# Four u tiles from TensorE to the DMA crossbar, an earlier attention, and one load held back

## The chip, the cores and the metric

One core of a Trainium2 chip. The metric is the device time of one execution in microseconds (us), the median of several runs; each run is listed with its mean granted TensorE clock. A run over 1.5% above the fastest of its kernel counts as slow. A ratio is the mean time of one kernel's fast runs over that of the other's in the same rounds, so it is not quite the ratio of the medians quoted.

## The reference, cut to what matters

```
q, k, v: (8 batches, 8 heads, 576 positions, 64), float32
scores = q k^T / 8, causal, window of 64 positions; attn = softmax(scores); x = attn v      # (8, 576, 512)
h = x^T U V (rank 32);  u = x + h^T;  out = u + relu(u w_ch1) w_ch2                         # w_ch1: 512 x 2048
```

## The kernel before

The 4608 tokens are worked on in nine chunks of 512. Each chunk has 32 slots: slots 0 to 15 hold the first matrix product (`ch1`, one group of 16 x 128 hidden columns each), slots 16 to 31 the second (`ch2`). Into the slots of chunk c the kernel puts the attention and the low-rank part of batch c+1. `ch1` reads u transposed (`uTc`), so each 128 x 512 tile of u must be transposed before the next chunk begins: on TensorE for batches under `NXT`, else by the DMA crossbar, issued from SyncE.

```python
NXT = 3
...
def UT(t):                                   # transpose u tile t of batch b
    def f():
        g = g0 + t
        dst = uT_of(g // TPC)[:, g % TPC, :, :]
        if b >= NXT:
            nc.sync.dma_start_transpose(out=dst, in_=u_tiles[g][:])
            return
        tp = ps_tp.tile([P, NDC, P], BF16, name="tpu", tag="tp")
        for dc in range(NDC):
            nc.tensor.transpose(tp[:, dc, :], u_tiles[g][:, dc * P : (dc + 1) * P], ident[:])
        nc.scalar.copy(out=dst, in_=tp[:])
...
def loads(b, *tiles):                        # GpSimd: wait, then load V and K/Q
    for t in tiles:                          # reads tile t of batch b+1's transposed Q: waits until it has landed
        nc.gpsimd.tensor_copy(out=held[:], in_=qfs[(b + 1) % 2][0:1, t * HP * P : t * HP * P + 1])
    if b <= 2:
        load_v(b + 1)
    for _ in load_kq(b + 2, False):
        pass
...
if 2 < b and b + 1 < B:                      # head of chunk b-1
    if b > 3:
        nc.gpsimd.tensor_copy(out=held[:], in_=uT_of(c)[0:1, TPC - 1, 0, 0:1])
    load_v(b + 1)
if 2 < b and b + 2 < B:
    loads(b, 2)
...
CROSS = {0: {2: [16, 17, 18, 19, 20]}, 1: {3: [10, ..., 14], 4: [26, ..., 30]}, 2: {5: [24, ..., 28]}}
CROSS_N = [22, 23, 24, 25, 26]               # slots of the crossbar transposes of K/Q, per chunk and batch
```

All loads go out on GpSimd's queue in program order, all crossbar transposes and stores on SyncE's, in program order too.

The softmax here doesn't subtract the row's maximum and nothing guards it: scores larger than these inputs give would overflow.

## Time and profile before

| | before |
|---|---|
| median of the first runs | 311.0 us (310.54 to 311.38) |
| span of the profiled run | 310.6 us |
| TensorE busy / DMA in use | 97% / nearly full to about 200 us |
| chunk 1, chunk 2, chunk 3, chunk 4 (from the chain in order of time) | 33.37, 31.95, 31.83, 31.62 us |

The lines are in the prediction. The digits of the page are tenths busy in 40 slices of the span; in the busy times by stretch each engine has its busy us and, in brackets, its instructions. Names: `kr`, `qr` are the loaded K and Q, `kf`, `qf` the same transposed, `vA`, `vB` V; `un` is a u tile, `uTc` u transposed, `tpu` its transpose on TensorE; `psA`, `psU` are the first and second matrix product in PSUM. PE is TensorE, PEld its weight loads, DVE VectorE, ACT ScalarE, POOL GpSimd, SPq SyncE's queue.

### The profile page before, as it was taken

What the parts mean: (1) busy time and instruction counts of PE and PEld (TensorE: products, weight loads), DVE (VectorE), ACT (ScalarE), POOL (GpSimd) and SP (SyncE); (2) the same over time, 40 slices, a digit from 0 to 9 for tenths busy, and PEclk for the clock granted to TensorE, in tenths of its full rate; (3) what the DMA queues carried; (4) which work ended last, traced back from release to release, by engine and by line L of the source; (5) the groups of instructions that cost most, each with busy time, mean ns of one, the idle gap of its engine ahead of it and who ended that gap; (6) DMA issues with size and microseconds to landing.
All of it is one profiled execution on the core that took longest, in us unless ns stands there. A gap on an engine that the chain in (4) does not pass through costs nothing.

```text
span 310.6 us, 6952 instructions
## 1 busy us (share of the span) xinstructions
PE 301.8 (97%) x2881; PEld 147.6 (48%) x2903; DVE 175.1 (56%) x336; ACT 108.2 (35%) x173; POOL 102.0 (33%) x136
## 2 busy tenths in 40 slices
PE   7799999999999999999999999999999999999996
PEld 7453554544545544454445444544454444444443
DVE  4485566528667873677557765666566542116011
ACT  3555680358127620543044304440354004101500
POOL 8693264294695091437143705000000000000000
PEclk9999999999999999999999999999999999999999
DMA  7999999999999999999599999932400275011011
GB/s 107 170 209 208 204 172 145 147 148 160 138 148 157 139 142 203 130 156 172 103 150 141 184 118 132 175 103 74 132 2 0 68 222 203 32 69 36 0 65 70
DMA packets 156495, 39.87 MB, mean 128 GB/s; under 512 B 145040, under 2 KB 151440, under 8 KB 156464
## 3 DMA queue, kind: packets, MB, share of 16 engines
q0 software_dynamic: 104720, 18.88, 82.0%
q1 hardware_dynamic: 51744, 20.55, 34.0%
q8 instruction: 22, 0.36, 0.5%
q14 instruction: 9, 0.07, 0.1%
HBM read 37.97 MB, written 9.44 MB: 153 GB/s over the span
## 4 chain that ended last, share of the span: by engine, by line
PE 93%; DMA 3%; issue 1%; DVE 1%; POOL 1%; ACT 0%; POOLq 0%
PE psA L765 41%; PE psU L789 40%; DMA qr<-in_q_dram 3%; PE sc L347 3%; PE xw L409 2%; PE psv L660 2%; PE pshh L533 1%; PE tpu L694 1%; PE tpg L283 1%; PE low L347 0%; PE psh L533 0%; DVE xs L420 0%; POOL kr L120 0%; PE tpw L283 0%; PE xe L409 0%
## 5 line engine op out<-in xcount | busy, mean ns | idle before, releaser
L765 PE MATMUL psA<-uTc,w1b 128*128 128x512 bf16 (+1 forms) x584 | 131.2, 377 | 0.3 <-DVE uTc L635 0.3
L789 PE MATMUL psU<-w2b,c 128*128 128x512 bf16 (+2 forms) x572 | 127.3, 373 | 1.3 <-issue 0.3
L789 PEld LDWEIGHTS <-c 128*128 128x128 bf16 x592 | 56.0, 98 | 66.0 <-issue 2.9
L765 PEld LDWEIGHTS <-w1b 128*128 128x128 bf16 x584 | 54.3, 98 | 63.9 <-issue 2.6
L777 ACT ACTIVATE c<-psA 128x512 bf16<-128x512 f32 x84 | 50.1, 597 | 83.6 <-PE psA L765 83.3
L775 DVE TENSOR_SCALAR c<-psA 128x512 bf16<-128x512 f32 x60 | 41.3, 689 | 40.9 <-PE psA L765 40.9
L802 DVE TENSOR_TENSOR osb<-psU,un 128x512 f32<-128x512 f32 (+2 forms) x29 | 19.5, 671 | 52.4 <-PE psU L789 52.4
L367 ACT ACTIVATE pts<-sc 128x1024 bf16<-128x1024 f32 x32 | 31.3, 1028 | 2.3 <-PE sc L347 2.3
L138 POOL DMA_DIRECT2D vA<-in_v_dram x32 | 28.3, 913 | 7.4 <-DMA w1b<-in_moe_w_ch_dram 2.7
L675 DVE TENSOR_TENSOR un<-psv,xs 128x512 bf16<-128x512 f32 (+3 forms) x48 | 26.1, 593 | 4.3 <-PE psv L660 4.0
L129 POOL DMA_DIRECT2D qr<-in_q_dram x30 | 26.7, 888 | 4.1 <-PE tpg L283 1.7
L129 POOL DMA_DIRECT2D kr<-in_k_dram x30 | 26.6, 887 | 3.4 <-PE sc L347 2.0
L400 ACT ACTIVATE ptl<-low 128x256 bf16<-128x256 f32 x6 | 2.3, 384 | 61.0 <-PE high L347 61.0
L373 DVE TENSOR_TENSOR pts<-pts,maskA 128x1024 bf16<-128x1024 bf16 x28 | 19.1, 682 | 1.7 <-ACT pts L367 1.7
L500 DVE TENSOR_TENSOR xs<-xw,rcw 128x896 bf16<-128x896 f32 x14 | 15.3, 1091 | 0.5
L963 POOL COPY held<-qf 1x1 bf16<-1x1 bf16 x5 | 0.9, 178 | 42.9 <-DMA qf<-qr 42.9
L347 PEld LDWEIGHTS <-kf 64*64 64x64 bf16 x704 | 9.8, 107 | 7.3 <-issue 7.0
L347 PE MATMUL sc<-qf,kf 64*64 64x128 bf16 (+1 forms) x608 | 11.5, 212 | 0.5 <-DVE qf L300 0.3
L409 PEld LDWEIGHTS <-pts 128*64 128x64 bf16 x512 | 9.8, 110 | 3.5 <-issue 2.5
L697 ACT COPY uTc<-tpu 128x512 bf16<-128x512 bf16 x9 | 5.3, 586 | 11.4 <-PE tpu L694 11.4
L409 PE MATMUL xw<-vA,pts 128*64 128x65 bf16 x217 | 8.4, 195 | 0.0
L974 POOL COPY held<-uTc 1x1 bf16<-1x1 bf16 x3 | 0.5, 177 | 23.6 <-DMA uTc<-un 23.6
(125 smaller groups left out, 190.7 us busy)
## 6 DMA issues: line engine op xcount, KB each, us to landing
out_dram<-osb SPq DMA_DIRECT2D x27, 256.0 KB, 2.3
vA<-in_v_dram POOLq DMA_DIRECT2D x32, 128.0 KB, 6.4
kr<-in_k_dram POOLq DMA_DIRECT2D x24, 128.0 KB, 5.4
qr<-in_q_dram POOLq DMA_DIRECT2D x24, 128.0 KB, 5.5
w2b<-in_moe_w_ch_dram POOLq DMA_DIRECT2D x4, 512.0 KB, 15.8
out_dram<-late SPq DMA_DIRECT2D x8, 256.0 KB, 4.2
vB<-in_v_dram POOLq DMA_DIRECT2D x8, 128.0 KB, 8.8
w1b<-in_moe_w_ch_dram POOLq DMA_DIRECT2D x2, 512.0 KB, 11.1
```

The lines of the kernel that those rows point to most:

```text
L129: nc.gpsimd.dma_start(out=dst[0:rows, t, :, :], in_=src[b, :, t * P : t * P + rows, :].rearrange("h p d -> p h d"),)
L138: nc.gpsimd.dma_start(out=dst[:, :, 0:D], in_=v[b, :, lo : lo + P, :].rearrange("h p d -> p h d"))
L347: nc.tensor.matmul(sc[g][r0 : r0 + W, col * W : (col + n) * W], keys_of(j, u, rs), queries_of(j, blk, n, rs), start=not spare, stop=last o ...
L367: nc.scalar.activation(out=dst, in_=sc[:], func=ACT.Exp, scale=scale)
L373: nc.vector.tensor_tensor(out=dst, in0=dst, in1=maskA.rearrange("p g n w -> p g (n w)"), op=ALU.mult)
L409: nc.tensor.matmul(dst, pts[:, h // 2, h % 2, blk, :] if blk < NB - 1 else ptl[:, h // 2, h % 2, :], rhs, start=True, stop=True,)
L675: nc.vector.tensor_tensor(out=u_tiles[g][rs, cs], in0=ps[0][n][rs], in1=x[rs, t, :, :].rearrange("p h d -> p (h d)")[:, cs], op=ALU.add,)
L765: nc.tensor.matmul(ps[i][:, ts.start * P : ts.stop * P], w1b[:, dc, i * P : (i + 1) * P], uTc[:, ts, dc, :], start=(dc == 0), stop=(dc == ...
L775: nc.vector.tensor_relu(out=c1[i][:], in_=ps[i][:])
L777: nc.scalar.activation(out=c1[i][:], in_=ps[i][:], func=ACT.Relu)
L789: nc.tensor.matmul(acc[t][:, lo:hi], c1[i][:, t * P : (t + 1) * P], w2b[:, i, lo:hi], start=(i == 0), stop=(i == NFC - 1),)
L802: nc.vector.tensor_tensor(out=osb[:, lo:hi], in0=acc[t][:, lo:hi], in1=u_tiles[g][:, lo:hi], op=ALU.add,)
```

## The change

Intent: take TensorE work off the bound (four u tiles go through the crossbar), make u of batch 2 ready soon enough for a crossbar transpose to land, and keep the DMA engines free for it by holding V of batch 3 back. The diff, whole but for line numbers:

```diff
+    XUT = ((1, 4), (2, 0), (2, 1), (2, 3))
-                if b >= NXT:
+                if b >= NXT or (b, t) in XUT:
-    DVE_RELU = {0: (7, 9, 11, 15), 1: (4, 7, 9, 10, 11, 13, 14)}
+    DVE_RELU = {0: (7, 9, 11, 15), 1: (3, 6, 8, 9, 10, 12, 13)}
-                parts = (slice(0, TPC - 1), slice(TPC - 1, TPC)) if c in (1, 2) and ids == (0,) else (slice(0, TPC),)
+                parts = (slice(0, TPC - 1), slice(TPC - 1, TPC)) if (c, ids) == (1, (0,)) else (slice(0, TPC),)
     PLACE_2 = {
-        "S": [9, 9, 9, 12, 12],  "M": [9, 10, 11, 13, 14], "SV": [15, 15, 16, 16], "PV": [18], "U": [23], "V": [25], "UT": [28, 29, 30, 31],
+        "S": [8, 8, 8, 11, 11],  "M": [8, 9, 10, 12, 13],  "SV": [13, 13, 14, 14], "PV": [15], "U": [20], "V": [22], "UT": [23, 23, 28, 25],
-                slots[15].append(lambda: loads(2, 2))
+                slots[15].append(lambda: loads(2, NT - 1))
```

(The lines of `PLACE_2` are put together here.) The last edit is the hold: GpSimd issues V of batch 3, and behind it K/Q of batch 4, once the last tile (4) of batch 3's K/Q has been transposed, no longer tile 2.

## The prediction

> **What bounds the kernel now.** I read the page's busy shares and slices first, then the chain that ended last, then who TensorE waited for, and last the clock times of the GpSimd and SyncE queues in the stretch that the change touches.
>
> From the page of the kernel before (busy share of the span; then tenths busy in 40 slices; then shares of the chain):
>
> ```profile
> PE 301.8 (97%) x2881; PEld 147.6 (48%) x2903; DVE 175.1 (56%) x336; ACT 108.2 (35%) x173; POOL 102.0 (33%) x136
> ...
> PE   7799999999999999999999999999999999999996
> ...
> DMA  7999999999999999999599999932400275011011
> ...
> PE 93%; DMA 3%; issue 1%; DVE 1%; POOL 1%; ACT 0%; POOLq 0%
> ```
>
> TensorE is the bound: 97% busy, 93% of the chain. The DMA engines are a second, hidden load: full up to about two thirds of the span. So a saving has to be TensorE time, and what could eat it is a transfer that lands late.
>
> The program works on nine chunks of 512 tokens, each of 32 slots: 16 slots of the first matrix product, 16 of the second, with the attention of the next batch (chunk c carries batch c+1) put in between. From the chain in order of time, chunk 1 begins at 60.3 us, chunk 2 at 93.7, chunk 3 at 125.66. The busy times by stretch (us of the stretch, then busy us of PE, PEld, DVE, ACT, POOL; clock; DMA share; GB/s):
>
> ```profile
> 60.30:93.70 33.40, 33.10 (x325) 16.29 (x326) 19.50 (x39) 14.77 (x24) 26.08 (x32) 1.00 2.00 145
> 93.70:125.66 31.96, 31.86 (x306) 15.22 (x306) 20.15 (x38) 12.54 (x20) 14.84 (x20) 1.00 1.85 156
> 157.50:189.10 31.60, 31.50 (x301) 14.84 (x302) 21.36 (x38) 10.28 (x16) 12.15 (x17) 1.00 1.39 146
> ```
>
> Chunk 1 takes 1.8 us more than chunk 4 (157.5 to 189.1), and TensorE is idle for only 0.3 us of it. It is longer because it has more TensorE work: the u tiles of batches 1 and 2 are transposed on TensorE there, while from batch 3 on they go through the DMA crossbar. In the whole of chunk 1 the waits of TensorE come to one entry:
>
> ```profile
> PE psU L789 <- issue: 0.2, 1, 0.2
> ```
>
> What one such transpose costs on TensorE is in its timeline at the end of chunk 1 (start us, us, what):
>
> ```profile
> 90.06 0.39 PE L694 MATMUL tpu<-ident,un 128*128 128x128 bf16 x4
> 90.28 1.03 PE L789 MATMUL psU<-w2b,c 128*128 128x512 bf16 x4
> 91.15 0.39 PE L694 MATMUL tpu<-ident,un 128*128 128x128 bf16 x4
> ...
> 93.54 1.04 PE L765 MATMUL psA<-uTc,w1b 128*128 128x384 bf16 x8
> ```
>
> The 0.39 is the latency of four pipelined matmuls; what counts is from start to start: 90.28 - 90.06 = 0.22 us for the tile, and 91.15 - 90.28 = 0.87 for the four matmuls after it.
>
> **What the Trainium skill says.** "TensorE: Matmul & The Clock Gate", section "Back-to-back issue gap", gives 134 cycles for 128 columns and 518 for 512 on a warm array, at 2.4 GHz about 56 and 216 ns. The trace agrees: 0.22/4 = 55 ns and 0.87/4 = 217 ns, at a granted clock of 1.00. "VectorE: DVE Perf Modes", section "The three transpose paths", puts 128x128 at 390 ns on TensorE and 1309 ns by the crossbar. The first is an isolated latency, and misleads here, where it is 55 ns of a stream. The second is near the 1.2 us that SyncE spends on issuing one crossbar transpose here, but that is a whole 128x512 tile; to its landing it takes 2.4 to 9.0 us (median 5.3 for the K/Q tiles). "DMA: Bandwidth & Descriptors", section "Issuing engines are not separate DMA queues", says that all issuers share the same 16 DMA engines. The trace fits: the crossbar transposes of K/Q land in a median of 5.3 us in the crowded part, those of u, mostly later, in 2.5.
>
> **The change part by part.**
>
> 1. Four u tiles leave TensorE: batch 1's last (chunk 1, slot 2) and batch 2's tiles 0, 1 and 3 (slots 28, 29, 31). All lie on the bound: 4 x 0.22 = **0.88 us saved**. ScalarE loses four copies of 586 ns (2.3 us), which is off the path, as it is 35% busy.
>
> 2. The first matmul group of chunk 2 is no longer split into 384 and 128 columns. Split, it takes from 93.54 to 94.51 until the scores begin (0.97 us); chunk 3's unsplit one from 125.49 to 126.45 (0.96). **0.01 us: nothing.**
>
> 3. Batch 2's attention comes sooner in chunk 1: scores by 1 slot, the V shifts by 2, P·V, U and V by 3. This moves work and removes none. The slots have about 0.865 us each (four matmuls), so the scores would come at about 69.3 - 0.9 - 0.2 (the transpose that is gone) = 68.2. The last crossbar transpose of batch 2's K/Q was issued at 61.16 and landed at 66.27: 1.9 us early. Batch 2's V landed by 69.5, and its first shift moves to slot 13, about 73.6: 4 us early. VectorE and ScalarE have idle time here (19.5 and 14.8 of 33.4 us), and the ReLUs given to VectorE move one slot with the scores. P·V now follows the last shift by one slot instead of two: ScalarE has two score exponentials (1.95 us), three shift copies (1.67) and two ReLUs (1.2) from about 71.9, so it is through at about 76.7, while P·V begins at 75.3. The shifted tile that it needs late could cost 0.1 to 0.3 us. I take **0.1**.
>
> 4. The new transfers have to land. SyncE and GpSimd in the kernel before:
>
> ```profile
> 81.02 1.48 SPq L306 DMA_TRANSPOSE kf<-kr  x1
> 82.59 1.22 SPq L306 DMA_TRANSPOSE qf<-qr  x1
> 90.91 1.20 SPq L306 DMA_TRANSPOSE kf<-kr  x1
> ...
> 79.97 0.18 POOL L963 COPY held<-qf 1x1 bf16<-1x1 bf16 x1 [6.96 <-DMA qf<-qr]
> 80.50 3.52 POOL L138 DMA_DIRECT2D vA<-in_v_dram  x4 [0.36 <-issue]
> ```
>
> SyncE is free from 83.8 to 90.9, between batch 3's and batch 4's K/Q. The additions that make u end, in the kernel before, at 89.98, six in 3.1 us from 86.84; so tile 0 would be ready at about 88.2 and tile 1 at 88.9. Three slots and one transpose sooner is 2.8 us: 85.4 and 86.1. SyncE then issues tile 0 at 85.4, tile 1 at 86.7, tile 3 at 88.0 (1.3 us apart, as its rows of K/Q are). Chunk 2, which reads tiles 0 and 1, begins at 93.54 - 0.88 = 92.7 (tile 3 belongs to chunk 3 and has 30 us more). How long does the landing take? Transposes of this stretch were issued at 79.71, 81.02 and 82.59 and landed 3.3, 5.3 and 5.95 us later, growing as V's loads (from 80.50) fill the DMA queues. Now V is held until the last K/Q transpose (issued at 82.6, about 3.1 us to land when nothing is beside it), so it starts at about 86.2. Tile 0 lands at about 88.7. Tile 1, issued 0.5 us after V's start, as the 81.02 one was, lands at about 86.7 + 5.3 = 92.0: **0.7 us before it is needed**. That is thin: with 6 to 7 us it would hold TensorE up by a fraction of a us to 1 us. I take 0.25 us as the mean. Batch 1's tile is issued about 62.4 and has 30 us.
>
> 5. What is held back. V of batch 3 is issued 5.7 us later (86.2 to 90), lands at about 90 to 96 (4 to 6 us), and is wanted in chunk 2 at slot 5, about 99 to 100: 4 us early. K/Q of batch 4 come 5.7 us later, so their transposes run from about 97 to 113 instead of 90.9 to 107.5. In the kernel before SyncE then stood idle for 6 us until batch 3's u was ready at 113.5, so most of the delay is taken up there. Batch 3's u then landed for chunk 3 by 122.5, 3.1 us before chunk 3. **Nothing on the path.** A 6 us delay in a full DMA may use that margin up, but most of the bytes moved are the same.
>
> Sum: -0.88 - 0.01 + 0.1 + 0.25 = -0.54, so 311.0 - 0.5 = 310.5; if all lands in time and P·V does not wait it is 310.1. I put the prediction between, at **310.3 us**, because the two penalties are likelier absent than present.
>
> **The rivals.**
>
> A, all lands in time: 310.1. For it: the change frees the DMA exactly where the transposes run, and TensorE has almost no wait in this part now. Against: the 0.7 us margin of tile 1.
>
> B, the transpose trades for a wait: chunk 2 begins with TensorE waiting for tile 1. For it: DMA is full (a share of 2.00, so on the view's scale no slack), landings up to 8 us are seen from 90.9 on. Against: V is held for that. It would give back 0.5 to 1.5 us: 310.6 to 311.6.
>
> C, the delay runs on: K/Q of batch 4, V of batch 4 and u of batch 3 each slip by some us, and chunk 3 begins late by 1 to 3 us, which makes 311 to 313. Against: the 6 us idle time of SyncE before batch 3's u.
>
> D, the earlier attention collides with the ReLUs: ScalarE or VectorE late with a drain, TensorE out of PSUM banks for 0.3 to 1 us: 310.4 to 311.1. Against: both were idle for over 13 us of the chunk.
>
> **Range and chances.** A has about half, B a quarter, D and C together a quarter. Runs of the kernel before lie 0.84 us apart, which widens all of this: 309.5 to 311.5. The whole TensorE work that goes is 0.3% of the time, so over 2% faster (below 304.8) can't come from it; over 2% slower (above 317.2) would need a stall of over 7 us, more than any margin above is likely to be missed by. Chances: faster 0.01, within 2% 0.97, slower 0.02.
>
> **What would show it.** Right: 20 instead of 36 transposing matmuls of u, 27 instead of 23 crossbar transposes of u; chunk 1 shorter by about 0.9 us, the later chunks as before to 0.1; no TensorE wait for a DMA at the start of chunk 2; tile 1 of batch 2 landed at about 92. Wrong: a gap before chunk 2's first matmul with the u transpose as its releaser (B), one before chunk 3's (C), or gaps around P·V at slot 15 (D). Wrong by its size if chunk 1 is shorter by clearly more or less than 0.88 us with no gap.

## The result, and the profile after

313.27 us median (312.73 to 313.84, four runs) against 310.92 (310.54 to 311.38, four runs): ratio 1.0075, interval 1.0049 to 1.0102. It is within 2%, slower by 2.3 us, and outside the range of 309.5 to 311.5.

From the page of the changed kernel, the same rows as of before:

```profile
PE 302.4 (97%) x2883; PEld 146.3 (47%) x2883; DVE 175.8 (56%) x336; ACT 106.2 (34%) x169; POOL 102.3 (33%) x136
...
PE   8889999999999998899989999999999999999995
...
DMA  7999999999999999999999999932400265010011
...
PE 87%; DMA 5%; DVE 3%; POOL 2%; issue 1%; SPq 1%; POOLq 0%
```

The busy share has not moved: 97%. The chain tells: TensorE fell from 93% to 87% of it, and DMA, VectorE and SyncE came in. The row of TensorE has 8s in the middle where there were only 9s.

Busy times by stretch of the changed kernel, chunks 1, 2 and 3:

```profile
59.46:91.75 32.29, 32.27 (x311) 15.39 (x310) 19.03 (x38) 13.22 (x21) 17.36 (x22) 1.00 1.70 134
91.75:125.69 33.94, 31.96 (x302) 14.76 (x301) 22.01 (x39) 11.95 (x19) 21.49 (x27) 1.00 2.17 136
125.69:158.62 32.93, 31.74 (x302) 14.77 (x303) 21.14 (x38) 10.28 (x16) 13.45 (x18) 1.00 1.79 168
```

Chunk 1 is 1.08 us shorter (33.37 to 32.29), as wanted. Chunk 2 is 1.99 longer and chunk 3 1.10, chunk 4 0.21; the rest of the span 0.16; the stretch before chunk 1 0.88 shorter. The sum, 1.5 us, is the difference of the two spans (312.1 and 310.6). The medians differ by more, 2.3, because the profiled run of the kernel before was a long one. It took 312.56 us, more than any of its timed runs; TensorE waited 1.6 us for Q in it (at 11 us), and chunk 1 began 0.88 us later than in the profile of the changed kernel. The waits below (3.0 us) less the saving of 0.88 make 2.1. TensorE's busy time in chunks 2 and 3 is what it was (31.96 and 31.74 beside 31.86 and 31.73), so these are waits. Who TensorE waited for from 91.7 to 160 us (us in total, times, longest):

```profile
PE psA L766 <- issue: 1.8, 1, 1.8
PE psA L766 <- DMA uTc<-un: 1.2, 1, 1.2
```

Both are the first matmul of a chunk. The second says that it waits for the crossbar transpose of u. The first, before chunk 3, is put down to "issue", but the third tile of batch 3's u landed at 125.60 us and the matmul started at 125.69. In the kernel before it had landed at 122.5.

GpSimd's queue (POOL) and SyncE's (SPq) show where the delay began; timelines, start and duration in us:

```profile
86.98 0.18 POOL L964 COPY held<-qf 1x1 bf16<-1x1 bf16 x1 [13.71 <-DVE late L803]
87.52 3.52 POOL L139 DMA_DIRECT2D vA<-in_v_dram  x4 [0.36 <-issue]
...
91.86 0.93 POOL L130 DMA_DIRECT2D kr<-in_k_dram  x1
```

```profile
98.05 1.19 SPq L307 DMA_TRANSPOSE kf<-kr  x1
...
113.43 1.34 SPq L307 DMA_TRANSPOSE qf<-qr  x1
114.87 1.71 SPq L691 DMA_TRANSPOSE uTc<-un  x1
```

V of batch 3 goes out at 87.5 instead of 80.5, K/Q of batch 4 at 91.9 instead of 84.85, their transposes run from 98.05 to 114.8 instead of 90.9 to 107.5. Only then can SyncE issue batch 3's u: at 114.87, while the first tiles' data were ready from about 112 on. The third tile landed 3.1 us later than before: it was issued 2.25 us later (119.28, not 117.03; 1.3 of this is the later start) and took 6.3 instead of 5.5 us. TensorE wanted it at 123.9 instead of 125.66, 0.9 us of that by the change and 0.9 by a sooner start of this run. So a margin of 3.1 us became a wait of 1.8.

Before chunk 4 the chain of the changed kernel is (start, us, what):

```profile
150.04 1.25 SPq L691
...
151.34 7.15 DMA uTc<-un
...
158.62 1.02 PE psA L766 x4
```

The transpose was issued as early as in the kernel before (its four from 149.89), but took 7.15 us to land instead of 2.4. What is new beside it are the loads of batch 6's K/Q: the trace has them issued from 141.2 to 152.8 and landing from 150.7 to 162, in the kernel before issued from 136.9 to 145.3, with the last recorded landing at 148.7. The last of these loads on GpSimd's queue, in the changed kernel and, below the dots, in the kernel before:

```profile
152.11 0.69 POOL L130 DMA_DIRECT2D qr<-in_q_dram  x1
...
144.52 0.76 POOL L129 DMA_DIRECT2D qr<-in_q_dram  x1
```

### The profile page after: what moved, and what is told of

It reads as the page before. It is cut to its first block, busy times and chain, and to the rows that moved or that the text cites.

```text
span 312.1 us, 6938 instructions
## 1 busy us (share of the span) xinstructions
PE 302.4 (97%) x2883; PEld 146.3 (47%) x2883; DVE 175.8 (56%) x336; ACT 106.2 (34%) x169; POOL 102.3 (33%) x136
## 4 chain that ended last, share of the span: by engine, by line
PE 87%; DMA 5%; DVE 3%; POOL 2%; issue 1%; SPq 1%; POOLq 0%
PE psA L766 40%; PE psU L790 37%; DMA vA<-in_v_dram 3%; PE sc L348 3%; DMA uTc<-un 2%; PE xw L410 2%; PE psv L661 1%; DVE un L676 1%; PE pshh L534 1%; DVE c L776 1%; DVE osb L803 1%; PE tpg L284 0%; POOL qr L121 0%; PE low L348 0%; PE psh L534 0%
## 5 line engine op out<-in xcount | busy, mean ns | idle before, releaser
L130 POOL DMA_DIRECT2D qr<-in_q_dram x30 | 26.0, 865 | 5.3 <-DMA w2b<-in_moe_w_ch_dram 2.8
L803 DVE TENSOR_TENSOR late<-psU,un 128x512 f32<-128x512 f32 x8 | 5.4, 686 | 6.3 <-PE psU L790 6.2
L139 POOL DMA_DIRECT2D vB<-in_v_dram x8 | 7.3, 909 | 4.7 <-DMA qr<-in_q_dram 2.5
```

The costliest lines, as they stand in the source:

```text
L130: nc.gpsimd.dma_start(out=dst[0:rows, t, :, :], in_=src[b, :, t * P : t * P + rows, :].rearrange("h p d -> p h d"),)
L139: nc.gpsimd.dma_start(out=dst[:, :, 0:D], in_=v[b, :, lo : lo + P, :].rearrange("h p d -> p h d"))
L803: nc.vector.tensor_tensor(out=osb[:, lo:hi], in0=acc[t][:, lo:hi], in1=u_tiles[g][:, lo:hi], op=ALU.add,)
```

## The experiments

The theories. **H**: the hold costs the time, as it delays V and K/Q. **X**: added crossbar transposes cost by themselves. **B**: without the hold batch 2's u would be late for chunk 2. After the first four runs a theory **M** took the place of H: each transposed u has a margin before its chunk; hold, added transposes and the saved TensorE time each take a part of it, and loads that fall beside the u transposes decide.

Of six the result is not the reference's, see e9. Ratios are to the kernel before in the same rounds.

| run | what it is | median us | ratio, 95% interval |
|---|---|---|---|
| e1 | changed, no hold | 315.44 | 1.0111 (1.0071 to 1.0151) |
| e2 | before + hold | 311.82 | 1.0014 (0.9981 to 1.0048) |
| e3 | before + sooner attention | 311.5 | 0.9998 (0.9964 to 1.0032) |
| e4 | changed, u tiles on TensorE | 312.19 | 1.0025 (0.9983 to 1.0068) |
| e5 | changed, tiles both ways | 313.19 | 1.0066 (1.0046 to 1.0086) |
| e6 | changed, V of batch 3 not held | 314.2 | 1.0097 (1.0071 to 1.0123) |
| e7, e15 | two slack tiles, no hold | 310.43, 310.38 | 0.9998 (0.9958 to 1.0039), 0.9985 (0.9966 to 1.0004) |
| e8 | changed again | 313.08 | 1.0073 (1.0034 to 1.0113) |
| e12 | changed, hold at tile 3 | 313.76 | 1.0073 (1.0048 to 1.0099) |
| e17 | changed + K/Q 5, 6, 7 held behind u | 310.23 | 0.9976 (0.9964 to 0.9989) |
| e18 | before + the same holds | 312.09 | 1.0047 (1.001 to 1.0083) |

**e1, the hold undone.**

```diff
-                slots[15].append(lambda: loads(2, NT - 1))
+                slots[15].append(lambda: loads(2, 2))
```

> The changed kernel with one part undone: V of batch 3 is issued once tile 2 of batch 3's K/Q is transposed, as in the kernel before. Theory H (the hold costs it: V of batch 3 and with it K/Q of batch 4 go out 7 us later, so batch 4's transposes end on SyncE at 114.8 instead of 107.5, batch 3's u lands after chunk 3 wants it, and K/Q of batch 6 then fall on batch 4's u): TensorE does not wait before chunks 3 and 4 (1.8 and 1.2 us now), and the time is 310.9 - 0.9 = 310.0. Rival X (the four added crossbar transposes delay the queue themselves): the waits stay, 312.5 to 313.5. Rival B (without the hold, batch 2's u lands late for chunk 2): a wait of 0.5 to 2 us at the start of chunk 2, 310.5 to 312.

H fell: the kernel became slower still, 315.44. B is what happened. TensorE's timeline at the start of chunk 2:

```profile
89.63 1.67 PE L790 MATMUL psU<-w2b,c 128*128 128x512 bf16 x7
94.83 0.92 PE L766 MATMUL psA<-uTc,w1b 128*128 128x512 bf16 x2 [3.53 <-DMA uTc<-un]
```

Tile 1 of batch 2 was issued at 87.3 and landed at 94.6 (7.3 us); in the changed kernel issued at 87.0, landed at 89.5 (2.5 us). So the hold does what it is for. The time is above B's 310.5 to 312: the wait was 3.5 us, and TensorE's clock was at half for 3.41 us after it (see e9).

**e2, the hold alone**, the same edit the other way in the kernel before.

> The kernel before with the hold alone (V of batch 3 waits for tile 4 of batch 3's K/Q, not tile 2). Theory H: K/Q of batch 4 go out about 6 to 7 us later and TensorE waits before chunk 3, now with chunk 2 starting 0.9 us later than in the changed kernel, so the wait there is about 1 us, and about 1.2 before chunk 4: 312.5 to 313.5. Rival X: 310.9, unchanged.

A miss: 311.82, ratio 1.0014, not told apart from no change. The mechanism is there, its size is not: batch 4's K/Q transposes began at 96.5 instead of 90.9, batch 3's third u tile landed at 123.4, wanted at 124.6, and TensorE waited 0.2 us in all before chunk 4. There batch 4's first u tile took 6.9 us to land instead of 2.4, so the hold alone puts K/Q of batch 6 beside it; the margin was just enough.

**e3, the sooner attention alone** (`PLACE_2` and `DVE_RELU` of the change but `UT` at 28 to 31, `XUT = ()`, no hold).

> The kernel before with batch 2's attention sooner alone (scores, shifts, P.V, U and V at the changed slots and the ReLUs moved with them; all u tiles on TensorE at the slots before; no hold). Theory H: nothing but order moves, 310.9 +- 0.3. Rival D (the sooner attention collides with the ReLUs): 311.5 or more, with TensorE waits in chunk 1.

As expected: 0.9998, and no wait of over 0.2 us from chunk 1 on. Rival D of the prediction is out for this part alone.

**e4, the changed kernel with its u tiles on TensorE** (`XUT = ()`, `UT` at 28 to 31, the split of chunk 2's first group back).

> The changed kernel with all four u tiles back on TensorE (sooner attention and hold kept). Theory H says more than that the hold costs time: the start of chunk 3 is then set by the DMA chain, so TensorE work before it is free, and putting back 0.88 us makes the wait before chunk 3 shorter by about as much: 313.3 +- 0.4, the same as the changed kernel. If the parts simply add, it is 313.3 + 0.9 = 314.2.

312.19: below both numbers. Sooner attention and hold together cost 0.25% (not certain), so by the means two thirds of the 0.75% come with the crossbar tiles, though the intervals overlap. Hold and sooner attention are cheap without them; and the tiles need the hold (e1).

**e5, the tiles both ways**: as the changed kernel, and the same four transposed on TensorE into PSUM that nobody reads.

```diff
+        def UD(t): ...    # four nc.tensor.transpose of u tile t into ps_tp, no copy out
+                place(b, ("UD",), {"UD": [29, 30, 31]})     # batch 2; batch 1's tile at once
```

> The changed kernel, and the four tiles are transposed on TensorE as well (at slots 2, 29, 30, 31 of chunk 1, into PSUM, read by nobody). So the DMA work is that of the changed kernel and the TensorE work that of the kernel before. The first four runs made the hold alone nearly free (311.8) and the hold without crossbar tiles 312.2, so the theory is now M, a margin: batch 3's u had 3.0 us before chunk 3 wants it; the hold takes some 2 of it, the crossbar tiles 2 more, and the TensorE time saved moves the want 1 us sooner; only all together cross zero. Theory M: chunk 3 starts when u lands, about 125.6 in a span that starts alike, whatever TensorE does before, so the added 0.88 us only shortens the wait from 1.8 to 0.9: same time as the changed kernel (e8) within 0.3. If saved TensorE time is worth itself: e8 + 0.9.

313.19 beside 313.08 of e8: **0.88 us of TensorE work put back costs nothing** that these runs can tell. But the intervals are some 0.2 and 0.4% wide to each side, so the difference of the two is uncertain by some 1.4 us, and a cost of 0.88 is not excluded by the times. The traces speak for theory M: 36 transposing matmuls are there again, and TensorE's waits from chunk 1 on are 1.5 us in all, beside 2.7 in e8 and 3.0 in the first profile. So what the change saved on TensorE was probably not on the path any more.

**e8, the changed kernel again.**

> The changed kernel once more, on the chip of these runs: 313.3 +- 0.6, a ratio to before of about 1.0075, TensorE waits of about 1.8 and 1.2 us before chunks 3 and 4. All theories say the same; it is the yardstick for the other three.

The same ratio, but other waits. TensorE's waits in its profile, from chunk 1 to 200 us:

```profile
PE psA L766 <- DMA uTc<-un: 1.5, 1, 1.5
PE low L348 <- DMA qf<-qr: 1.2, 1, 1.2
```

The first is before chunk 4. Before chunk 3 there is none this time (u landed 124.1, wanted 124.6), but the sooner scores of batch 2 waited for its K/Q, the last of which landed at 68.3 instead of 66.3. So which margin is missed differs from run to run; the sum is 2.7 us here and 3.0 in the first profile.

**e6, V of batch 3 out at once** behind batch 3's K/Q, only K/Q of batch 4 held.

```diff
-                if b <= 2:
+                if b <= 1:
                     load_v(b + 1)
                 for _ in load_kq(b + 2, False):
                     pass
+                if b == 1:
+                    load_v(3)
```

> The changed kernel, with V of batch 3 issued at once behind batch 3's K/Q (about 73 to 77, into DMA time of which a part is free at 78 to 82) and only K/Q of batch 4 held until batch 3's K/Q are transposed. Theory M: K/Q of batch 4 go out at about 88 instead of 91.9, their transposes end 3 to 4 us sooner, batch 3's u lands by about 122.5 and there is no wait before chunks 3 and 4: 310.2. Rival: V of batch 3 delays batch 3's K/Q transposes, and with them batch 2's u (wanted at 91.6): a wait before chunk 2 of 0.5 to 3 us and 311 to 313.

A failed repair: 314.2. V beside the K/Q transposes made these end at 91.5 instead of 86.8, so that nothing was gained behind them, and 1.9 us of wait stood before chunk 4.

**e7 and e15, only the tiles that have time.** `XUT = ((1, 4), (2, 3))`, `UT` at 28, 29, 30, 25, no hold, the rest of e3. These two tiles are read 30 us later.

> Only the two tiles that are wanted 30 us later go through the crossbar (batch 1's last, batch 2's tile 3); tiles 0 and 1 of batch 2 stay on TensorE, no hold, sooner attention kept. Theory M: the DMA chain is that of the kernel before plus two transposes (under 1 us of the 3.0 us margin), so 0.44 us of TensorE time is really saved: 310.9 - 0.4 = 310.5 if before runs 310.9. Rival X (any added crossbar transpose costs by itself): 311.5 or more.

> The two slack tiles alone once more (e7: five runs of 309.7 to 311.0 and one of 314.0 at a clock of 0.989). Theory M: 0.44 us of TensorE work less and no wait, ratio 0.998 to 0.999; now and then a run whose margin is missed by 2 us or more, which also shows a lower granted clock.

e7 had five runs of 309.7 to 311.0 and one of 313.97 (clock 0.989); e15 gave 310.38 and 0.9985. Rival X is out for these two tiles: a crossbar transpose costs nothing just by being added. No wait was over 0.2 us from chunk 1 on. The gain is of the size expected (0.44 us is 0.14%), but both intervals include no change. The run of 313.97 was not profiled, so its cause is not known.

**e12, a weaker hold** (`loads(2, 3)`).

> The changed kernel with a weaker hold: V of batch 3 waits for tile 3 of batch 3's K/Q instead of tile 4 (about 2 us sooner). The hold trades a wait before chunk 2 (3.5 us without it, 0 with it) for waits before chunks 3 and 4. Theory M: a mixture, some 0.5 to 1.5 us before chunk 2 and 1 to 2 us later on; 313 to 314.5, no better than the full hold. If the hold itself were the cost, it would be better than the full hold: 312 or less.

313.76, no better: 1.9 us before chunk 2 (tile 1 landed at 93.3) and 0.5 before chunk 4. The hold moves the wait about; it doesn't make it.

**e9 and e10, loads kept off the u transposes.** GpSimd reads one element of batch 4's (e10: and batch 3's) transposed u of the next chunk before it issues K/Q of batch 6 (e10: and 5).

```diff
-            if 2 < b and b + 2 < B:
+            if 2 < b and b + 2 < B and b not in (4,):          # e10: (3, 4); e13, e16, e17, e18: (3, 4, 5)
                 loads(b, 2)
...
+            if b in (4,):
+                def behind_u(b=b, c=c):
+                    nc.gpsimd.tensor_copy(out=held[:], in_=uT_of(c + 1)[0:1, TPC - 1, 0, 0:1])
+                    loads(b, 2)
+                slots[22].append(behind_u)                      # e17, e18: slots[21]
```

> The changed kernel with one thing: K/Q of batch 6 are not issued before batch 4's u has landed for chunk 4 (they are wanted a chunk later). In the changed kernel their loads (issued 139 to 149) land from 149 to 158, beside batch 4's u transposes (issued 149 to 152, landing 7.2 us later instead of 2.4). Theory M, last link: those transposes then land in 2.4 to 4 us, the wait before chunk 4 (1.2 to 1.5 us) goes, and the time is 313.1 - 1.4 = 311.7. Rival S (the transposes are late because SyncE or the additions come late, not because of the loads beside them): landings stay at 7 us and the wait stays, 313.1.

> As e9, and K/Q of batch 5 held too until batch 3's u has landed for chunk 3 (they go out at about 123 instead of 115). Theory M: both waits go, 310.2 to 311. Rival: V and K/Q of the later batches now slip further and a wait shows in chunk 4 or 5: 312 or more.

**A fault of mine.** At slot 22 the first crossbar transpose of batch 6 already stands ahead of its loads, so tile 0 of batch 6's K/Q (from e13 on also of batch 7) was that of two batches before. The comparison passed it, as the scores are small: computed from the reference, such a swap in both batches changes their outputs by 0.9% in norm. e9, e10, e11, e13, e14 and e16 have it. What comes before batch 6's K/Q are transposed (up to chunk 4's start) is not touched; later times may be.

e9 says this of the links. Batch 4's u, issued at 152.6, landed in 2.4 us and the wait before chunk 4 was gone, as expected; S fell. But a wait of 3.2 us before chunk 3 was in that profile, and a wait before chunk 5 had come, where K/Q of batch 7 now fell beside batch 5's u:

```profile
PE psA L766 <- issue: 3.2, 1, 3.2
PE psA L766 <- DMA uTc<-un: 1.7, 1, 1.7
```

The median was 314.74 (with the one slow run, 318.96; the fast ones took 312.8 to 316.7), ratio 1.0089: as a repair it failed. With K/Q of batch 5 held too (e10, 312.28, 1.0017, the rival's forecast) the waits before chunks 3 and 4 were both gone and only one of 1.7 us was left, before chunk 5.

The wait before chunk 3 in e9 shows one thing more. Busy times by stretch around it (the last four columns are POOL's busy time, the granted clock, DMA share and GB/s):

```profile
123.40:126.60 3.20, 0.02 (x1) 0.02 (x1) 0.69 (x1) 0.00 (x0) 1.10 (x2) 1.00 1.86 160
126.60:130.00 3.40, 3.38 (x60) 1.80 (x61) 1.12 (x2) 2.03 (x4) 1.94 (x3) 0.66 1.57 224
130.00:133.00 3.00, 3.00 (x43) 1.34 (x44) 2.35 (x4) 0.71 (x2) 0.88 (x1) 0.81 1.55 175
```

After 3.2 us without work the clock is 0.66 and 0.81 for a while; the trace has half clock from 127.71 to 131.12, 3.41 us. Chunk 3 then took 33.16 us without any wait, against 31.56 in e13: a long wait costs some 1.6 us a second time. The Trainium skill, "TensorE: Matmul & The Clock Gate", section "Part 1: The HAM clock gate", states half rate after an idle window of about 3.4 us; the trace agrees on the half rate, though the gap of 3.2 us was shorter than that. One such stretch costs 3.41/2 = 1.7 us, 0.5% of the span. The three profiled runs with a clock of 0.995 (e1, e9, e11) each have one, after waits of 3.5, 3.2 and 2.5 us. The other stray long runs have clocks of 0.995 or 0.989, which would fit one or two such stretches, but they were not profiled.

**e11, e13, e14, e16**, the same holds with the two slack tiles (e11: K/Q 6; e14: K/Q 6 and 7), in the changed kernel (e13) and in the kernel before (e16), all with the fault.

> The version with only the two slack tiles on the crossbar (e7, 310.4 median), and K/Q of batch 6 held as in e9. e7 had no wait left at chunks 3 and 4, so theory M says that the hold of K/Q 6 changes nothing there but takes away the spread of its margin: 310.4 +- 0.3, ratio to before about 0.998. If holding loads back is bad in itself: 311.5 or more.

> The changed kernel with K/Q of batches 5, 6 and 7 each held until the u of batches 3, 4 and 5 has landed for the next chunk. Theory M (the loads issued beside the u transposes are what makes them late): no TensorE wait of over 0.5 us before any chunk and 0.9 us of TensorE work saved against before: ratio to before 0.997 to 0.999. Rival (other causes of lateness remain: SyncE order, V loads): waits of 1 us or more somewhere, ratio 1.003 or more.

> The two slack tiles on the crossbar, no hold of V, K/Q 6 and 7 held behind u. e11, with K/Q 6 alone held, had a wait before chunk 5 of 2.5 us. Theory M: it goes, ratio 0.998 to 0.999 (0.44 us of TensorE work less).

> The kernel before with the same three holds and nothing else. It has no wait before chunks 3 to 5, so theory M says no gain: ratio 0.999 to 1.001. If the holds are good by themselves: 0.997 or less, and then e13 does not speak for the cause.

e11 was a miss, 313.88 (1.0076), with 2.5 us before chunk 5, where K/Q of batch 7 fell beside batch 5's u: moving a load off one chunk's u put it on the next one's. e13 was 310.24 (0.998), e14 310.11 (0.9974), e16 310.7 (0.9993), none with a wait of 0.5 us after chunk 1. Because of the fault I rest nothing on these.

**e17 and e18, the same holds one slot sooner**, in the changed kernel and in the kernel before; these compute the reference.

> As e13 (the changed kernel, K/Q of batches 5, 6, 7 held until u of batches 3, 4, 5 has landed), with the loads one slot sooner, so that they stand ahead of their own transposes. Theory M: no TensorE wait of over 0.5 us before chunks 2 to 6 and a ratio to before of 0.996 to 0.999. Rival: SyncE's transposes of batch 6 and 7 now wait for these loads and hold up what is behind them; a wait of 1 us or more before chunk 5 or 6, ratio 1.002 or more.

> Control: the kernel before with the same holds in the right order. Theory M: no wait to take away, so a ratio of 0.999 to 1.001, and e17 is faster than it by the TensorE time saved, 0.5 to 0.9 us. If the holds help by themselves it is 0.997 or less.

e17: 310.23 (five runs), ratio 0.9976, **faster than the kernel before and, by the ratios to it, than the changed one.** GpSimd's queue shows the new waits, here the second (the loads of K/Q 6 now begin at 154.24):

```profile
153.51 0.18 POOL L1009 COPY held<-uTc 1x1 bf16<-1x1 bf16 x1 [16.21 <-DMA uTc<-un]
```

All that TensorE waited for from 59 to 200 us, and chunks 1 and 2 (a stretch each):

```profile
PE psU L790 <- issue: 0.2, 1, 0.2
```

```profile
59.80:92.00 32.20, 31.96 (x311) 15.32 (x310) 19.17 (x38) 13.22 (x21) 17.23 (x22) 1.00 1.65 134
92.00:124.10 32.10, 31.89 (x301) 14.94 (x302) 20.50 (x38) 11.95 (x19) 15.00 (x20) 1.00 1.96 146
```

Chunk 1 keeps its saving and chunk 2 is at 32.1 instead of 33.94. The control e18 was not faster: three of its runs are at full clock, 310.4 to 311.5, as before, and three at 0.995 to 0.989, 312.7 to 314.4. That half is a miss: the holds can make a wait elsewhere in the kernel before, which its one profile, of a fast run, doesn't show. So the control shows no gain of the holds in themselves; in the changed kernel they give the change room. Whether e17 would now and then have such long runs too, five runs can't tell.

The margins, from the issue and landing of each transfer in the traces (us; one profile each, positive is early). Wanted is when the chunk's first matmul started or, where it had to wait, when TensorE was through with the chunk before. (The chain's 125.66 above is the end of the last matmul of chunk 2, which overlaps the start at 125.5; hence 3.1 there and 3.0 here.)

| | u of batch 3 (third tile): landed, wanted, margin | u of batch 4 (second tile): landed, wanted, margin |
|---|---|---|
| before | 122.5, 125.5, +3.0 | 153.6, 157.3, +3.7 |
| e3 sooner attention | 123.8, 125.0, +1.2 | 153.1, 156.6, +3.5 |
| e4 and hold | 123.2, 124.9, +1.7 | 157.1, 156.6, -0.5 |
| changed | 125.6, 123.9, -1.7 | 158.5, 157.4, -1.1 |
| e8 changed again | 124.1, 124.6, +0.5 | 157.7, 156.4, -1.3 |
| e5 tiles both ways | 124.2, 124.1, -0.1 | 157.2, 156.0, -1.2 |
| e17 | 121.3, 124.1, +2.8 | 153.4, 155.7, +2.3 |

The hold takes the margin of batch 4's u (4 us of it, from e3 to e4). Of batch 3's, 1.8 us are already gone with the sooner attention alone (before to e3), part of it because the profile of the kernel before began chunk 1 0.8 us later than that of e3. What the crossbar tiles add shows less cleanly: from e4 to the changed kernel and its repetition the margins shrink by 0.6 to 3.4 us, part of it because TensorE comes sooner.

## Why the prediction was wrong

1. **TensorE's saving** (step 1): right in chunk 1, which lost 1.08 us against 0.88 predicted; 20 transposing matmuls and 27 crossbar transposes of u are in the trace, as foreseen. The difference of 0.2 is no more than between two runs (e2 has the TensorE work of before, and its chunk 1 took 33.1 us instead of 33.37). e17 ends 0.5 us under the kernel before.
2. **The split** (step 2): nothing was seen of it; it was not tested alone.
3. **The sooner attention** (step 3): free by itself (e3). The penalty of 0.1 us around P·V was not seen in the changed kernel's chunk 1. But that K/Q would land 1.9 us before the sooner scores was wrong: in the first profile they landed at 67.11, 0.8 us later than before, and the scores came at 67.35, 0.85 sooner than foreseen, so 0.24 us was left, and no wait was luck. In e8 they landed at 68.3, and TensorE waited 1.2 us; e4 and e9 show waits of 0.3. Why K/Q land later is not shown.
4. **Tile 1 of batch 2** (step 4): foreseen to land at 92.0, 0.7 us early; it landed at 89.5. I had V's loads begin at 86.2 beside it; they began at 87.5, after it was issued. Its landing without the hold, 7.3 us in e1, was just above my 6 to 7. Rival B was thus no danger in the changed kernel, but the main one without the hold. Two readings given for B were wrong: landings from 90.9 on go up to 9.0 us, not 8, and a DMA share of 2.00 is not the top of the view's scale (chunk 2 of the changed kernel has 2.17, a stretch of e11 2.73).
5. **What is held back** (step 5): this is the step that failed. "Nothing on the path" was wrong. The delay of K/Q of batch 4 was 7.0 us, not 5.7; SyncE's idle time took up most of it, as I wrote, but the third tile behind it landed 3.1 us later where the margin was 3.1 and the want came 1.8 sooner: a wait of 1.8 before chunk 3. The margin was also read from one run, whose chunk 1 had begun 0.9 us later than in the changed kernel's; e3, with no hold, has only 1.2. And I followed the delay for one batch only: it ran on through K/Q of batch 5 (first issue 115.75, not 108.2) to K/Q of batch 6, whose loads then lay beside batch 4's u: a wait of 1.2 before chunk 4. The runs show that link: with them off it, u lands in 2.4 (e9) to 4.4 us (e17) instead of 7.2, and that wait is gone. With K/Q of batch 5 off batch 3's u as well, its third tile lands in 3.7 us instead of 6.3 (e17), and the wait before chunk 3 is gone too.

Rival C was named, "chunk 3 begins late by 1 to 3 us, 311 to 313"; it came, with 1.8 us and a total of 313.27, just above its range, and with a second wait before chunk 4 that it did not name. It had been given too little weight beside the pull of the saved 0.88 us. The sum had treated saved TensorE time as a gain for sure; the waits in e5 and e17 suggest that it was worth nothing here until the DMA margins were restored.

What stays open: how much of the 0.75% is hold and how much crossbar (the intervals of e4 and the changed kernel overlap), why K/Q of batch 5 take up to 16 us to land in the changed kernel and 4 to 6 in the kernel before (no run was aimed at it), and where e18's slow runs wait.

## What to carry to other kernels

When the bound engine is 97% busy beside a DMA that is nearly full, list for every transfer when it lands and when it is wanted before taking work off the bound: that work may be what the margins consist of. A load that is held back delays everything behind it in its queue, so follow the delay until a margin takes it up, two or three stages on, and look at what it comes to lie beside. Work moved to the crossbar is cheap for tiles that are wanted late (e7, e15), and for urgent ones, in this kernel, only with bulk loads kept off their landing (e17).

## What the Trainium skill lacked or had wrong

- "VectorE: DVE Perf Modes", section "The three transpose paths": it compares 390 ns on TensorE with 1309 ns by the crossbar for 128x128. For a choice like this one the numbers that decide are others: 55 ns in a stream on TensorE, and for a whole 128x512 tile by the crossbar 1.2 to 2.5 us of issue and 2.4 to 7.7 us to landing.
- "TensorE: Matmul & The Clock Gate", section "Back-to-back issue gap", which the prediction cites: it gives the 134 and 518 cycles as the gap of an isolated matmul, and for a stream of weight loads and matmuls about 81 ns at 128 columns and 131 ns at 512. The prediction left this out. The stream in this trace has 55 and 217 ns, so here the figures called isolated hold and those for a stream don't.
- "DMA: Bandwidth & Descriptors", section "Issuing engines are not separate DMA queues": it says that all transfers interleave, but not how much a crossbar transpose suffers. Beside loads issued from GpSimd a 128x512 transpose took 7.15 us (batch 4's u, changed kernel) and 7.3 us (batch 2's, e1) to land; with these loads held off, batch 4's took 2.4 to 4.4 (e9, e17) and batch 2's 2.5 (changed kernel).
- "TensorE: Matmul & The Clock Gate", section "Why this matters for your kernels": it advises no idle gaps over about 3 us. In the profiles here a gap of 2.5 us (e11) was already followed by half clock for 3.41 us, one of 1.9 us (e12) was not.
